# Causal attention scores at 64-key granularity: first half-blocks of two heads stacked in one score tile

## The chip, the cores and the metric

The kernel runs on one core of one Trainium2 chip. The metric is the device time of one execution in microseconds (us), the median over the runs of one kernel. The kernel before took 278.13 to 278.65 us in four runs. Every record calls its runs "fast", so all runs here are compared as they are; but runs of some changed kernels differ in their mean granted clock (split8: 0.987 to 1.0), and that is taken up below. Engines are called by their profile names: PE is TensorE, PEld its weight loads, ACT is ScalarE, DVE is VectorE, POOL is GpSimd, SP is SyncE, which only issues DMAs here.

## The reference, cut to what matters

A sequence of 2048 tokens of width 512 is cut into 4 segments of 512. Each of 32 heads (16 wide) does causal softmax attention inside a segment, plus a linear "memory" over the earlier segments; a gated MLP of width 1792 runs beside it, and a gate mixes the two.

```python
for s in range(4):
    logits = einsum('bhqd,bhkd->bhqk', qs, ks) * 0.25 + mask      # causal, inside the segment
    a_dot  = softmax(logits) @ vs
    a_mem  = (phi(qs) @ M) / (phi(qs) @ z + 1e-6)                 # phi(t) = t+1 if t>0 else exp(t)
    o = g * a_mem + (1 - g) * a_dot
    M, z = M + phi(ks).T @ vs, z + phi(ks).sum()
a = concat(o) @ wo
b = (gelu(x @ w_gate) * (x @ w_up)) @ w_down
out = gx * a + (1 - gx) * b                                       # gx = sigmoid(x . gate_w)
```

## The kernel before

The kernel is a list of tasks. A list scheduler inside the program orders them with estimated durations (`est`) and hand-tuned priorities (`BIAS`); each engine then runs its own part strictly in that order, and waits on semaphores where it needs another engine. So a change of a task's engine or of a buffer's name can move the whole order.

Scores for one group `t` of eight heads (four row groups `g` of 32 rows, two heads `j` in each) are written to one PSUM tile of 128 keys x 4 x 512 columns. `kpad[j]` is K with the rows of the other head set to zero. A "fill" is one set of tiled matmuls into that tile; one ACT instruction then takes exp of all 2048 columns, and POOL zeroes what lies above the diagonal.

```python
R_PT = 7                                   # buffers for exp(scores)
def fill(name, steps, diags):              # ... cut
    for (j, kb, ncol, c0) in steps:        # kb: block of 128 keys; queries from the block on
        for g in range(4):
            X[g][:, c0:c0+ncol] = kpad[j][32*g:32*g+32, t, kb*128:(kb+1)*128].T @ qT[32*g:..., t, kb*128:512]
    PT[slot] = exp(XALL * 0.25)            # ACT, 128 x 2048
    affine_select(PT[slot] ...)            # POOL, 512 or 1024 elements a partition

a0 = fill("A0", [(0, 0, 512, 0)], [0])
b0 = fill("B0", [(0, 1, 384, 0), (0, 3, 128, 384)], [0, 384])
cc = fill("C",  [(0, 2, 256, 0), (1, 2, 256, 256)], [(0, 256)])
a1 = fill("A1", [(1, 0, 512, 0)], [0])
b1 = fill("B1", [(1, 1, 384, 0), (1, 3, 128, 384)], [0, 384])
pv(0, a0, b0, cc, joint); pv(1, a1, b1, cc, joint)    # 16 tiled matmuls each: P times [V | 1]
norm()                                                # DVE: divide, transpose, add
```

That is 5 fills for each of 16 groups, 80 in all. Between them PE runs the projections and the MLP, whose 512-column matmuls fill four PSUM banks that ACT and DVE must empty. Other DVE work: `phi` of q and k (bf16 `tensor_scalar` from SBUF to SBUF: `phq`, `kT`, `pex`), the padded copies of K, and the eviction of every MLP tile.

The softmax here doesn't subtract the row's maximum and nothing guards it: scores larger than these inputs give would overflow.

## Time and profile before

| | before |
|---|---|
| time, median of 4 runs | 278.25 us (278.13 to 278.65) |
| profiled span | 276.7 us |
| PE / ACT / DVE / POOL busy | 265.9 / 213.1 / 196.7 / 101.5 us |
| matmuls of 512 columns start apart | 0.216 us |

The page's head and its rows of 40 slices: a digit is the busy share of a slice in tenths, and PEclk is the granted PE clock.

```profile
span 276.7 us, 5333 instructions
PE 265.9 (96%) x2147; PEld 114.8 (41%) x2186; DVE 196.7 (71%) x336; ACT 213.1 (77%) x166; POOL 101.5 (37%) x197
...
PE   8999999999999999999999999999899999999995
...
PEclk9999999999999999999999999999999999999999
```

PE never rests for long. What a fill costs PE is read from starts in the timeline of PE (start us, length us, what):

```profile
102.57 0.59 PE L430 MATMUL psW<-xT,wq 128*128 128x512 bf16 x2
103.09 0.40 PE L741 MATMUL psXALL<-qT,kpad_1 32*128 32x384 bf16 x8
103.42 0.61 PE L430 MATMUL psW<-xT,wq 128*128 128x512 bf16 x2
```

The second of the two full matmuls started at about 102.78, the next full one at 103.42: 0.64 us, of which a normal matmul would have taken 0.216. The fill costs PE 0.42 us, though its 512 columns stream in about 0.21.

Groups of POOL and DVE instructions (busy us, mean ns of one, idle time before them):

```profile
L761 POOL TENSOR_SCALAR_AFFINE_SELECT pt<-pt 128x512 bf16<-128x512 bf16 x96 | 63.7, 664 | 141.7 <-ACT pt L749 119.7 <-ACT exs L645 19.3
L761 POOL TENSOR_SCALAR_AFFINE_SELECT pt<-pt 128x1024 bf16<-128x1024 bf16 x16 | 17.6, 1101 | 14.3 <-ACT pt L749 14.3
...
L606 DVE TENSOR_SCALAR pex<-pex 128x1024 bf16<-128x1024 bf16 x12 | 5.9, 488 | 0.0
...
L604 DVE TENSOR_SCALAR phq<-qT 128x1024 bf16<-128x1024 bf16 x6 | 3.2, 529 | 0.0
```

### The profile page before, as it was taken

The page shows a single profiled execution, that of the slowest core. Times are in us where ns is not written, and L with a number is a line of the kernel's source. Part 1 is how long each engine was busy: PE and PEld are TensorE (multiplying, and loading weights), DVE is VectorE, ACT ScalarE, POOL GpSimd, SP SyncE. Part 2 cuts the span into 40 slices and gives each one's busy share as a digit, 9 for nine tenths or more (in the row PEclk, how much of TensorE's full clock was granted, in tenths as well). Part 3 has the DMA queues.
Part 4 walks back from the last instruction along what each step waited for, and adds up shares of the span by engine and source line. Part 5 has one row for each costly group of instructions (what it writes and reads, how often), then busy time and mean ns, then how long its engine had stood idle before and what let it go on. Part 6 is the DMA issues. An engine that isn't in the chain of part 4 may idle for free.

```text
span 276.7 us, 5333 instructions
## 1 busy us (share of the span) xinstructions
PE 265.9 (96%) x2147; PEld 114.8 (41%) x2186; DVE 196.7 (71%) x336; ACT 213.1 (77%) x166; POOL 101.5 (37%) x197
## 2 busy tenths in 40 slices
PE   8999999999999999999999999999899999999995
PEld 3444344334454434444454444433344334433342
DVE  1589879977889669989727999868553669273534
ACT  3698889899989779877778988767868668677701
POOL 8465633431013342464205543443300433342410
PEclk9999999999999999999999999999999999999999
DMA  6999940000022431000201210410000000001002
GB/s 177 217 376 361 201 79 2 0 4 0 0 59 57 95 40 59 1 2 10 50 0 21 57 40 0 97 38 1 4 0 0 4 0 2 19 21 39 0 2 76
DMA packets 29697, 15.30 MB, mean 55 GB/s; under 512 B 21224, under 2 KB 29672, under 8 KB 29672
## 3 DMA queue, kind: packets, MB, share of 16 engines
q1 hardware_dynamic: 29672, 14.96, 22.4%
q8 instruction: 17, 0.28, 0.4%
q14 instruction: 8, 0.07, 0.1%
HBM read 8.14 MB, written 2.10 MB: 37 GB/s over the span
## 4 chain that ended last, share of the span: by engine, by line
PE 81%; ACT 6%; DVE 4%; POOL 2%; issue 2%; DMA 2%; SPq 1%; DVEq 0%; ACTq 0%; POOLq 0%
PE psW L430 65%; PE psXALL L741 8%; PE psW L774 6%; ACT pt L749 5%; DMA wq<-in_A_wq_dram 2%; PE psXALL L430 1%; POOL exsT L656 1%; SPq L461 1%; POOL pt L761 1%; DVE hT L873 1%; ACT L852 1%; DVE ost L901 1%; DVE tb L782 0%; ACT hT L852 0%; DVE ndsc L678 0%
## 5 line engine op out<-in xcount | busy, mean ns | idle before, releaser
L749 ACT ACTIVATE pt<-psXALL 128x2048 bf16<-128x2048 f32 x80 | 150.1, 1877 | 39.0 <-PE psXALL L741 23.8
L761 POOL TENSOR_SCALAR_AFFINE_SELECT pt<-pt 128x512 bf16<-128x512 bf16 (+1 forms) x112 | 81.1, 727 | 156.0 <-ACT pt L749 134.0
L430 PE MATMUL psW<-xT,wu 128*128 128x512 bf16 x216 | 51.3, 380 | 1.4 <-DVE hT L873 0.6
L430 PE MATMUL psW<-wd,hT 128*128 128x512 bf16 x199 | 50.3, 380 | 1.2 <-issue 1.0
L430 PE MATMUL psW<-xT,wg 128*128 128x512 bf16 x216 | 50.3, 380 | 1.1 <-issue 0.8
L873 DVE TENSOR_TENSOR hT<-psW,hT 128x512 bf16<-128x512 f32 x56 | 37.3, 685 | 15.2 <-PE psW L430 13.6
L782 DVE STREAM_TRANSPOSE tb<-psW 128x512 f32<-128x512 f32 x32 | 21.1, 697 | 21.6 <-PE psW L774 21.4
L430 PEld LDWEIGHTS psW<-xT,wg 128*128 128x128 bf16 x224 | 20.5, 98 | 25.9 <-issue 2.6
L430 PEld LDWEIGHTS psW<-xT,wu 128*128 128x128 bf16 x224 | 20.2, 98 | 25.7 <-issue 2.6
L430 PEld LDWEIGHTS psW<-wd,hT 128*128 128x128 bf16 x210 | 18.7, 98 | 22.9 <-issue 4.0
L852 ACT ACTIVATE hT<-psW 128x512 bf16<-128x512 f32 x28 | 16.0, 600 | 6.8 <-PE psW L430 6.8
L774 PE MATMUL psW<-pt,vaug 128*17 128x256 bf16 (+3 forms) x512 | 20.4, 300 | 0.2 <-ACT hT L852 0.2
L430 PE MATMUL psW<-xT,wq 128*128 128x512 bf16 x59 | 15.7, 380 | 0.8 <-DMA wq<-in_A_wq_dram 0.3
L430 PE MATMUL psW<-xT,wk 128*128 128x512 bf16 x63 | 16.3, 380 | 0.2 <-issue 0.2
L741 PE MATMUL psXALL<-qT,kpad_1 32*128 32x512 bf16 (+3 forms) x256 | 15.8, 301 | 0.5 <-ACT pt L749 0.5
L741 PE MATMUL psXALL<-qT,kpad_0 32*128 32x512 bf16 (+3 forms) x256 | 15.8, 301 | 0.0
L430 PE MATMUL psW<-wv,xT 128*128 128x512 bf16 x61 | 15.4, 380 | 0.2
L447 DVE CAST hT<-psW 128x512 bf16<-128x512 f32 x20 | 13.1, 680 | 3.4 <-PE psW L430 3.4
L430 PE MATMUL psW<-wo,oT 128*128 128x512 bf16 x57 | 15.1, 380 | 0.2
L656 POOL COPY exsT<-exs 32x4 f32<-32x4 f32 x64 | 13.8, 216 | 3.7
L774 PEld LDWEIGHTS psW<-pt,vaug 128*17 128x17 bf16 x512 | 10.7, 90 | 10.5 <-issue 3.5
L901 DVE TENSOR_SCALAR ost<-psW,omgt 128x512 bf16<-128x512 f32 x10 | 7.3, 748 | 9.8 <-PE psW L430 9.8
(90 smaller groups left out, 252.1 us busy)
## 6 DMA issues: line engine op xcount, KB each, us to landing
out_dram<-ost SPq DMA_DIRECT2D x16, 128.0 KB, 1.7
wg<-in_B_w_gate_dram SPq DMA_DIRECT2D x2, 896.0 KB, 6.9
wu<-in_B_w_up_dram SPq DMA_DIRECT2D x2, 896.0 KB, 11.1
wd<-in_B_w_down_dram SPq DMA_DIRECT2D x1, 1792.0 KB, 15.9
hT<-in_A_x_dram SPq DMA_DIRECT2D x2, 256.0 KB, 3.0
wv<-in_A_wv_dram SPq DMA_DIRECT2D x1, 512.0 KB, 6.4
wo<-in_A_wo_dram SPq DMA_DIRECT2D x1, 512.0 KB, 12.7
wk<-in_A_wk_dram SPq DMA_DIRECT2D x1, 384.0 KB, 5.0
```

What stands on the lines that cost most here:

```text
L430: return Instr(lambda e: e.matmul(view(), lhsT, rhs, start=first, stop=last), reads=reads, writes=[fkey if fkey is not None else g.key], e ...
L447: alts[DVE] = [Instr(lambda e: e.tensor_copy(dst(), src()), reads=reads, writes=writes, est=dve_t(n))]
L461: return e.dma_start(out_ap(), in_ap())
L656: cross = task(f"exsT{s}", POOL, [Instr(lambda e, g=g, c=c: e.tensor_copy(exsT[sl][32 * g:32 * g + 32, c:16:4], exs[32 * c:32 * c + 32, s4 ...
L741: instrs.append(Instr(lambda e, t=t, g=g, j=j, kb=kb, ncol=ncol, c0=c0: e.matmul(X[g][:, c0:c0 + ncol], kpad[j][sl][32 * g:32 * g + 32, t, ...
L749: prev_exp[0] = exp_task(s, f"exp{s}_{t}{name}", [Instr(lambda e: e.activation(PT[slot][:], XALL[:, :].rearrange("p (g c) -> p g c", g=4), ...
L761: minstrs.append(Instr(lambda e, view=view, pat=pat: e.affine_select(out=view, in_=view, compare_op=ALU.is_ge, fill=0.0, base=0, pattern=p ...
L774: instrs.append(Instr(lambda e, q=q, kb=kb, slot=slot, c0=c0, h=h: e.matmul(gp.f32()[32 * q:32 * q + 17, 128 * kb:512], Vaug[sl][:, kb, h, :],
L782: task(f"pvt{s}_{t}_{j}", DVE, [Instr(lambda e: e.transpose(Tb[:, j, :], gp.f32()[:, :]), [gp.key], [("Tb", j)], dve_t(512))], grp=gp)
L852: lambda e, g=g, ft=ft, s=s: e.activation(hT[s % 2][:, ft, :], g.f32()[:, :], ACTF.Gelu_apprx_tanh),
L873: task(f"Um{s}_{ft}", DVE, [Instr(lambda e, g=g, ft=ft: e.tensor_tensor(hT[sl][:, ft, :], g.f32()[:, :], hT[sl][:, ft, :], ALU.mult), [g.k ...
L901: DVE: [Instr(lambda e, view=view, gt=gt, tile=tile: e.tensor_scalar(ostage[tile][:], view(), omgt[:, gt:gt + 1], None, ALU.mult), rd, [(" ...
```

## The change

The intent is to waste fewer score columns. In the old fills, the first 64 queries of a 128-key block are computed against all 128 keys, though causality allows only the first 64. The change lets the row fills start at query 64 of each block, and gathers the left-out corners (64 keys x 64 queries) of two heads, stacked on 128 partitions, of all four blocks and of two groups `t` in one extra "low" fill. 4 x 16 + 8 = 72 fills instead of 80, so 72 exps of 2048 columns. For the low part, a second V operand `Vlow[j]` holds V of the first 64 keys on one half of the partitions and zeros on the other; a DMA brings it across partitions. Room for the new tiles comes from other buffers, and all priorities (`BIAS`) were tuned anew.

```diff
-R_PT = 7
+R_PT = 6
+N_OST = 3                                   # output stages, were 4
+    klow = sb("klow", [P, 4, 4, 2, 64])      # first 64 keys of each block, both heads, padded
-    pex = [sb(f"pex{i}", ...) for i in range(2)]
+    pex = sb("pex", [P, 2, 512])
+    Vlow = [sb(f"vlow{j}", [P, 4, 16, 17]) for j in range(2)]
-    otok = sb("otok", [P, 4, 512])           # obf and ott: also 2 -> 1
+    otok = sb("otok", [P, 2, 512])
+    PTl = sb("ptl", [P, 4, 512])             # exp of the low fill, one buffer
+        for j in range(2):
+            dma(f"Vlo{s}_{j}", SP, lambda j=j: Vlow[j][64*j:64*j+64], lambda j=j: Vaug[sl][0:64, :, j], ...)
+            def rows(j, kbs, name):          # key blocks (0,3) and (1,2): 448+64 and 320+192 columns
+                ... kpad[j] block kb x queries kb*128+64 .. 512; masks of 256 elements
+            def lows():                      # 2 groups x 4 blocks x 64 columns
+                masks = [(PTl[64 * h:64 * h + 64].rearrange("p g (b c) -> p (g b) c", c=64),
+                          [[0, 32], [1, 64]], 0, 2048) for h in range(2)]
+                fill("L", steps, PTl, ("PTl",), masks)
             def pv(...):                     # 16 matmuls of 448,320,192,64 columns
+                for kb in range(4):          # and 16 of 64 columns
+                    for q in range(4):
+                        ... Vlow[j][:, kb, 4*t+q, :] x PTl[:, q, 256*(t%2)+64*kb : +64]
-            a0, b0, cc, a1, b1 = five fills
+            for j in range(2):
+                at[j] = {**rows(j, (0, 3), f"A{j}"), **rows(j, (1, 2), f"B{j}")}
+                if j == 0 and t % 2 == 0:
+                    lows()
```

The mask of the low fill is two POOL selects, one for each half of the partitions, of 2048 elements each.

## The prediction

> **What bounds the kernel now.** TensorE. The page gives PE busy 265.9 of 276.7 us (96%), ACT 213.1, DVE 196.7, POOL 101.5. In the windows view only about 6 us of idle PE lie between 10 and 263 us. The chain of waits is 81% PE; where it passes through exp and masking (114 to 129, 246 to 253 us) PE is full of other matmuls. So the time is the sum of PE's start-to-start intervals plus a few us of stalls. ACT is the second limit: in the timeline the score tile cycles every 2.59 us (fill, exp of 1.877, fill), 80 x 2.59 = 207 us.
>
> **What changes, from start-to-start intervals in the trace.**
> - Fills. A fill among full matmuls takes 0.311 us from the last full start to its own and 0.329 to the next full one; less the 0.216 of a normal matmul it costs 0.424, with 4 matmuls or with 8. Half is a fixed price of switching. Eight fewer: -3.4 us. The 64 row fills keep 512 columns and 8 matmuls: unchanged.
> - The 8 low fills have 32 matmuls of 64 columns. Four tiled matmuls start 3 to 4 ns apart, which agrees with the Trainium skill, "TensorE: Matmul & The Clock Gate", Part 3 (about 4 ns), so four fit into the 27 ns that 64 columns stream. Part 1 puts a floor of about 25 ns under start-to-start; the trace agrees (one-column gate matmuls start 25 ns apart). 64 columns are just above it. Estimate: 3 to 10 ns extra per step, +0.2 to +0.6 us in all.
> - PV. 1280 columns per accumulation before and after; matmuls double, 512 to 1024. Steps of 512, 384, 256, 128 columns now take 222, 163, 109, 56 ns: streaming plus about 4. Four more steps: +15 to +50 ns for each of 32, +0.5 to +1.5 us.
> - PV runs that start after full matmuls, not behind a fill, fall from 4 to 2 in the instruction order: -0.6 us.
> - ACT: 8 exps fewer, -15 us; off the critical path, except that some of 2 to 3 us of mid-kernel PE stalls may go.
> - POOL: 112 masks (0.664 us for 512 elements, 1.10 for 1024) become 128 of 256 (estimate 0.44) and 16 of 2048 (estimate 2.0): 81 to 88 us. The low mask is two in a row, 4 us of latency before a pair's first PV.
> - DVE: klow copies, +5 us. DMA: 8 small copies of V. Six P tiles for seven, single low P and V buffers, three output stages: more possible waits. All off the critical path if the order has room.
>
> **Predicted time.** PE: -3.4 + 0.4 + 1.0 - 0.6 = -2.6 us. Stalls: even, give or take 2. About **275.6 us**, 8 in 10 between 272.8 and 279.2. Faster by over 2%: 0.09; within 2%: 0.85; slower: 0.06. The 15 us taken from ACT almost all become ACT idle.
>
> **What the profile should show.** PE 95 to 97% busy; ACT busy 198 to 200 us; 72 exps of 1.88; a fill still 0.42 us of PE, a low fill 0.42 to 0.51; a PV accumulation 0.56 to 0.60 us instead of 0.55, its short steps 29 to 37 ns; POOL 100 to 115 us; fill cycle still 2.6 us.
>
> **What would make it wrong.** Slower: short steps of 50 ns or more because weight loads can't keep up (+2.5 us or more for PV, +1.5 for low fills); PV waiting for the low mask or for the single low buffers, with PE standing; a copy of V blocking transposes behind it in the queue. Faster: stalls that vanish with ACT's new slack, up to 3 us more.

## The result, and the profile after

The changed kernel took 285.9 us (285.69 to 287.6, 4 runs) beside 278.25 us. Ratios in this document are the mean time of one kernel's runs over that of the other's of the same rounds, so not quite the ratio of the medians. Here it is 1.0286, with a 95% interval of 1.0245 to 1.0327: slower by 2.9%, and outside the predicted range. The output is correct.

The same lines of the page:

```profile
span 284.3 us, 6936 instructions
PE 264.7 (93%) x2913; PEld 120.8 (42%) x2954; DVE 196.8 (69%) x338; ACT 206.1 (72%) x170; POOL 115.1 (40%) x231
...
PE   8999859989999989999999969997999999999995
...
PEclk9999999999999999999999989997999999999999
```

PE has less busy time and a longer span: holes appear, and the clock row has two dips. From the matmul records, the gaps of PE above 0.5 us are one of 0.6 us before, and six after: 0.93 (at 28.9 us), 2.73 (36.9), 0.99 (60.1), 1.14 (104.4), 2.55 (164.4) and 1.78 (193.3), together 10.1 us.

The PE costs themselves were as predicted. A PV pair of the changed kernel:

```profile
72.35 0.61 PE L810 MATMUL psW<-pt,vaug 128*17 128x448 bf16 x16
72.79 0.29 PE L818 MATMUL psW<-ptl,vlow 128*17 128x64 bf16 x16
72.91 0.61 PE L810 MATMUL psW<-pt,vaug 128*17 128x448 bf16 x16
```

From start to start one accumulation takes 0.56 us; before it took 0.55. The steps of 64 columns run 29 ns apart (median), and a low fill costs 0.45 us of PE against 0.43 for a row fill (medians).

What changed is elsewhere. Groups of POOL and DVE (smaller and other groups between them are left out, here and below):

```profile
L768 POOL TENSOR_SCALAR_AFFINE_SELECT pt<-pt 128x256 bf16<-128x256 bf16 x128 | 57.4, 451 | 139.8 <-ACT pt L764 115.8 <-ACT exs L665 18.3
L768 POOL TENSOR_SCALAR_AFFINE_SELECT ptl<-ptl 64x2048 bf16<-64x2048 bf16 x16 | 34.5, 2157 | 9.7 <-ACT ptl L764 9.1
...
L612 DVE TENSOR_SCALAR pex<-pex 128x1024 bf16<-128x1024 bf16 x12 | 11.1, 924 | 4.5 <-ACT pex L607 4.5
L644 DVE TENSOR_SCALAR klow<-kT,maskc 128x1024 bf16<-128x1024 bf16 x6 | 6.5, 1131 | 0.0
L610 DVE TENSOR_SCALAR phq<-qT 128x1024 bf16<-128x1024 bf16 x6 | 5.8, 963 | 0.0
```

The very same `pex` and `phq` instructions take almost twice as long on average. The timelines of POOL and of DVE around the first gap show why:

```profile
23.58 4.42 POOL L768 TENSOR_SCALAR_AFFINE_SELECT ptl<-ptl 64x2048 bf16<-64x2048 bf16 x2 [0.69 <-ACT ptl L764]
```

```profile
24.36 1.68 DVE L610 TENSOR_SCALAR phq<-qT 128x1024 bf16<-128x1024 bf16 x1
25.96 2.33 DVE L612 TENSOR_SCALAR pex<-pex 128x1024 bf16<-128x1024 bf16 x1
28.33 0.77 DVE L614 TENSOR_TENSOR phq<-phq,pex 128x1024 bf16<-128x1024 bf16 x1
29.02 1.27 DVE L452 CAST hT<-psW 128x512 bf16<-128x512 f32 x2
```

The two selects ran from 23.584 to 25.755 and from 25.823 to 28.009 us. `phq` ended at 26.041 and `pex` at 28.292: each 0.28 to 0.29 us after the end of the select that was running when it started. Two such instructions at 161 to 165 us give the same 0.28 us. It is not `tensor_scalar` alone: a `tensor_tensor` between SBUF tiles (L845), 0.42 to 0.43 us elsewhere, took 1.47 us under a select at 190.1 us. The nine evictions from PSUM that ran wholly under a low select were not held: 677 to 692 ns, 690 elsewhere (median). But DVE runs in the order of its list, so the PSUM eviction behind the two came about 3 us late (1.27 and 1.92 us over the 0.41 of a free one), and PE stood for a bank (timeline of PE):

```profile
27.00 1.90 PE L435 MATMUL psW<-xT,wg 128*128 128x512 bf16 x8
29.84 0.59 PE L435 MATMUL psW<-xT,wg 128*128 128x512 bf16 x2 [0.93 <-DVE hT L452]
```

At 36.9 us PE waits for something else, the first copy of V:

```profile
36.31 0.61 PE L810 MATMUL psW<-pt,vaug 128*17 128x448 bf16 x16
39.66 0.29 PE L818 MATMUL psW<-ptl,vlow 128*17 128x64 bf16 x16 [2.73 <-DMA vlow<-vaug]
```

And after the gap at 164.4 us five full matmuls take 2.34 us, so 0.43 us apart, twice the normal 0.216. The windows view of that stretch, and of the one with the gap at 193.3 us (length in us; busy us and count of PE, PEld, DVE, ACT, POOL; mean clock; DMA share, GB/s) gives the clock as 0.90 and 0.89:

```profile
168.00 2.34 PE L435 MATMUL psW<-wo,oT 128*128 128x512 bf16 x5
```

```profile
155.00:172.00 17.00, 14.24 (x118) 5.84 (x114) 14.79 (x25) 11.47 (x10) 11.21 (x25) 0.90 0.16 32
185.00:200.00 15.00, 13.00 (x172) 5.70 (x163) 11.42 (x17) 8.71 (x6) 6.82 (x8) 0.89 0.15 38
```

The trace's clock record has two stretches of 3.413 us at half clock, which by our estimate cost about 1.7 us of PE work each (half of 3.413).

The longest gap, 2.73 us, brought no such stretch, so length alone does not decide. The clock record changes only on a grid of 3.413 us. On this grid, in all 14 profiles, each of the eleven full-clock windows in which PE stood for 1.78 us or more was followed by half clock, and no window with 1.68 us or less was. The 2.73 us fell across two windows, 1.36 and 1.38 us.

### The profile page after: what moved, and what is told of

The parts are those of the page before. It is cut to its first block, busy times and chain, and to the rows that moved or that the text cites. A ratio compares the mean times of both kernels' runs of the same rounds, so it can differ in the third digit from the quotient of the medians.

```text
span 284.3 us, 6936 instructions
## 1 busy us (share of the span) xinstructions
PE 264.7 (93%) x2913; PEld 120.8 (42%) x2954; DVE 196.8 (69%) x338; ACT 206.1 (72%) x170; POOL 115.1 (40%) x231
## 4 chain that ended last, share of the span: by engine, by line
PE 75%; DVE 15%; issue 3%; ACT 3%; POOL 2%; DMA 1%; SPq 0%; ACTq 0%; POOLq 0%
PE psW L435 60%; PE psXALL L757 7%; PE psW L810 5%; DVE hT L452 3%; DVE pex L612 3%; POOL exsT L676 2%; DVE phq L610 1%; PE psXALL L435 1%; ACT pt L764 1%; DVE klow L644 1%; PE psW L818 1%; PE psW L518 1%; DMA vlow<-vaug 1%; DVE phq L614 1%; DVE tb L825 1%
## 5 line engine op out<-in xcount | busy, mean ns | idle before, releaser
L764 ACT ACTIVATE pt<-psXALL 128x2048 bf16<-128x2048 f32 x64 | 120.1, 1876 | 44.3 <-PE psXALL L757 39.7
L768 POOL TENSOR_SCALAR_AFFINE_SELECT pt<-pt 128x256 bf16<-128x256 bf16 x128 | 57.4, 451 | 139.8 <-ACT pt L764 115.8
L435 PE MATMUL psW<-xT,wu 128*128 128x512 bf16 x216 | 53.1, 388 | 2.7 <-DVE otok L708 1.8
L435 PE MATMUL psW<-wd,hT 128*128 128x512 bf16 x201 | 49.1, 380 | 1.2 <-issue 1.1
L768 POOL TENSOR_SCALAR_AFFINE_SELECT ptl<-ptl 64x2048 bf16<-64x2048 bf16 x16 | 34.5, 2157 | 9.7 <-ACT ptl L764 9.1
L810 PE MATMUL psW<-pt,vaug 128*17 128x192 bf16 (+3 forms) x512 | 18.8, 273 | 0.0
L764 ACT ACTIVATE ptl<-psXALL 128x2048 bf16<-128x2048 f32 x8 | 15.0, 1876 | 3.1 <-PE psXALL L757 3.1
L435 PE MATMUL psW<-wo,oT 128*128 128x512 bf16 x54 | 16.2, 410 | 0.6 <-issue 0.5
L452 DVE CAST hT<-psW 128x512 bf16<-128x512 f32 x21 | 14.0, 681 | 1.9 <-PE psW L435 1.7
L612 DVE TENSOR_SCALAR pex<-pex 128x1024 bf16<-128x1024 bf16 x12 | 11.1, 924 | 4.5 <-ACT pex L607 4.5
```

The lines of the kernel that those rows point to most:

```text
L435: return Instr(lambda e: e.matmul(view(), lhsT, rhs, start=first, stop=last), reads=reads, writes=[fkey if fkey is not None else g.key], e ...
L452: alts[DVE] = [Instr(lambda e: e.tensor_copy(dst(), src()), reads=reads, writes=writes, est=dve_t(n))]
L612: Instr(lambda e: e.tensor_scalar(ex[:], ex[:], 1.0, None, ALU.min), [("pex",)], [("pex",)], dve_t(1024, 4)),
L764: prev_exp[0] = exp_task(s, f"exp{s}_{t}{name}", [Instr(lambda e: e.activation(dst[:], XALL[:, :].rearrange("p (g c) -> p g c", g=4), ACTF ...
L768: m = task(f"msk{s}_{t}{name}", POOL, [Instr(lambda e, view=view, pat=pat, base=base: e.affine_select(out=view, in_=view, compare_op=ALU.i ...
L810: instrs.append(Instr(lambda e, t=t, q=q, kb=kb, slot=slot, c0=c0: e.matmul(gp.f32()[32 * q:32 * q + 17, 128 * kb + 64:512], Vaug[sl][:, k ...
```

## The experiments

Theory A: a POOL select of 2.16 us holds off DVE's fast SBUF-to-SBUF instructions until it ends; DVE evicts late, PE stands, and the clock drops after some of the longer gaps. The Trainium skill, "SBUF — State Buffer", section "Who interferes with whom", says that VectorE and GpSimd share a pair of SBUF ports, that a VectorE instruction in a two-port mode contends for it, and that whoever comes first has it for the whole instruction. The trace agrees (1.68 and 2.33 us for instructions of 0.41). Rival B: the smaller number of buffers, and the V copy in the DMA queue.

Twelve kernels ran. All gave correct results. "Order unchanged" was checked by comparing the instruction lists of each engine. The diffs below are cut to what matters, and some are shortened in words.

| kernel | median us | range | ratio to before (95%) |
|---|---|---|---|
| changed kernel | 285.90 | 285.69 to 287.60 | 1.0286 (1.0245 to 1.0327) |
| split16 | 278.80 | 278.24 to 279.21 | 1.0010 (0.9992 to 1.0028) |
| split8 | 277.82 | 276.20 to 279.22 | 0.9974 (0.9922 to 1.0026) |
| before_lock | 285.64 | 284.12 to 285.74 | 1.0244 (1.0215 to 1.0273) |
| before_bufs | 324.24 | 323.45 to 324.80 | 1.1650 (1.1625 to 1.1674) |
| before_fixbufs | 283.73 | 283.52 to 283.83 | 1.0187 (1.0169 to 1.0204) |
| before_split | 277.66 | 277.29 to 277.79 | 0.9975 (0.9962 to 0.9988) |
| dvemask | 296.89 | 294.61 to 298.24 | 1.0647 (1.0611 to 1.0683) |
| dvemask_fix | 277.20 | 276.02 to 279.07 | 0.9968 (0.9936 to 0.9999) |
| split8_vlo | 277.64 | 275.29 to 279.39 | 0.9972 (0.9931 to 1.0013) |
| dvemask_vlo | 276.34 | 275.39 to 278.43 | 0.9941 (0.9908 to 0.9975) |
| after_q | 281.92 | 280.04 to 283.31 | 1.0128 (1.0088 to 1.0168) |
| dvemask_q | 273.91 | 272.82 to 274.01 | 0.9828 (0.9809 to 0.9847) |

### split8 and split16: the same masks in shorter pieces

```diff
-                masks = [(PTl[64*h:64*h+64].rearrange("p g (b c) -> p (g b) c", c=64),
-                          [[0, 32], [1, 64]], 0, 2048) for h in range(2)]
+                masks = [(PTl[64*h:64*h+64].rearrange("p g (b c) -> p (g b) c", c=64)[:, 8*i:8*i+8],
+                          [[0, 8], [1, 64]], 0, 0) for h in range(2) for i in range(4)]   # split16: 16 blocks, 2 pieces
```

The estimates keep their sum, so PE, DVE, ACT and SP run in the same order.

> The changed kernel with each of the 16 low masks (2048 elements, 2.16 us) cut into four of 512 elements; the order of instructions on every other engine is the same, and the POOL work is not less (about 0.66 us x 64 = 42 us for 34.5). Theory A (a long POOL instruction holds off the vector engine's fast SBUF-to-SBUF instructions for up to 2.3 us, evictions come late, TensorE stands): no such vector instruction over 1.3 us, TensorE's long gaps mostly go, 279 to 282 us. Rival B (fewer and single buffers, and the V copy in the queue): no gain, 285.5 to 288 us, since the low mask takes longer, not shorter.

> The same, each low mask cut into two of 1024 elements (1.1 us). Theory A: a dose between, 281 to 284 us, vector instructions held up to about 1.5 us. Rival B: 285.5 to 287 us.

POOL of split8, then its DVE `tensor_scalar` groups:

```profile
L768 POOL TENSOR_SCALAR_AFFINE_SELECT ptl<-ptl 64x512 bf16<-64x512 bf16 x64 | 45.5, 711 | 13.0 <-ACT ptl L764 9.0
```

```profile
L612 DVE TENSOR_SCALAR pex<-pex 128x1024 bf16<-128x1024 bf16 x12 | 7.5, 621 | 1.9 <-ACT pex L607 1.9
L610 DVE TENSOR_SCALAR phq<-qT 128x1024 bf16<-128x1024 bf16 x6 | 3.4, 568 | 0.0
```

POOL works 11 us longer on the low masks (45.5 for 34.5 us), and the kernel is 8.1 us faster. So it is the length of one POOL instruction that costs, not POOL's total and not the time until the low mask is done, which got longer (from the end of the exp mostly 4.4 to 5.0 us in the changed kernel, 5.8 to 7.0 here). Rival B alone cannot explain that. Both ranges were missed on the good side: even pieces of 1.22 us (split16) win back 7.1 us. In split8's profile PE's gaps above 0.5 us shrink to two, 2.01 us at 36.7 us and 0.68. Split8's four runs lie apart, 276.2 and 276.7 at a clock of 1.0, and 278.9 and 279.2 at 0.994 and 0.987: in half of the runs the clock still drops. The 2.01 us gap is the likely cause, though only one run has a trace: there it fell across two windows of the grid (0.33 and 1.68 us) and the clock stayed full.

### before_lock: the kernel before, with long POOL instructions added

```diff
+    scr = sb("scr", [P, 1536], mybir.dt.uint8)          # nothing else reads it; its memset is cut here
+                if name == "C" and t % 2 == 0:
+                    for _ in range(2):
+                        v = scr[0:64, :]
+                        minstrs.append(Instr(lambda e, v=v: e.affine_select(out=v, in_=v, compare_op=ALU.is_ge,
+                            fill=0.0, base=4096, pattern=[[1, 1536]], channel_multiplier=-1), [("scr",)], [("scr",)], 0.0))
```

> The kernel before with 16 extra POOL selects of 64 x 1536 bytes on a scratch tile that nothing reads, two after the C mask of every even head group, where the changed kernel has its low masks; nothing else moves in any engine's order. Theory A: fast vector instructions held for up to about 1.7 us, 280.5 to 285 us. Rival B: 278 to 279 us.

The 16 useless selects take 1.55 us each, and the kernel loses 7 us, a little over the 6.7 us that the expectation allowed. The same DVE group as above went from 488 to 735 ns:

```profile
L769 POOL TENSOR_SCALAR_AFFINE_SELECT scr<-scr 64x1536 uint8<-64x1536 uint8 x16 | 24.8, 1553 | 0.5
```

```profile
L608 DVE TENSOR_SCALAR pex<-pex 128x1024 bf16<-128x1024 bf16 x12 | 8.8, 735 | 0.0
```

Long POOL selects in those places are thus enough to cost 7 us, with no low fill, no V copy and all buffers in place. The half clock is not needed for it: the run at a clock of 1.0 took 285.58 us. The selects also hold up the real masks behind them in POOL's order, but the trace shows no stop of PE's matmuls over 0.1 us that ended with POOL, and PE's weight loads waited for POOL as long as before (1.2 us). The stops that ended with DVE went from 2.4 us in the kernel before to 7.1 us. The longest (timelines of POOL, DVE and PE):

```profile
89.36 3.25 POOL L769 TENSOR_SCALAR_AFFINE_SELECT scr<-scr 64x1536 uint8<-64x1536 uint8 x2
```

```profile
89.61 1.68 DVE L608 TENSOR_SCALAR pex<-pex 128x1024 bf16<-128x1024 bf16 x1
91.32 1.83 DVE L610 TENSOR_TENSOR kT<-kT,pex 128x1024 bf16<-128x1024 bf16 x1
```

```profile
93.81 0.41 PE L431 MATMUL psW<-mzbd,phq 128*128 128x128 bf16 x4 [1.98 <-DVE otok L690]
```

### before_bufs and before_fixbufs: the buffers alone

```diff
-R_PT = 7
+R_PT = 6
+N_OST = 3
-    pex = [sb(f"pex{i}", [P, 2, 512]) for i in range(2)]
+    pex = sb("pex", [P, 2, 512])                        # and otok 4 -> 2, obf and ott 2 -> 1
```

> The kernel before with the changed kernel's buffer counts only: 6 P tiles, 3 output stages, one exp buffer for q and k, two token tiles, single normalisation tiles. Theory A: 278 to 280.5 us. Rival B (buffers cost it): 283 us or more.

It took 324 us, which answers nothing: with other buffers the scheduler made another order. In its chain of waits PE runs 154 plain matmuls without a break from 25.97 us, and then stands between exps:

```profile
25.97 30.85 PE psW L431 x154
...
62.02 1.89 ACT pt L750
63.95 0.50 PE psXALL L742 x4
64.53 1.89 ACT pt L750
```

The repair keeps the old order and renames the buffers only after scheduling, when the waits are made. The old order has two `pex` tiles in flight at once, so that one stays double.

```diff
+    def phys(k):                                        # after scheduling, before the waits are planned
+        if k[0] in ("obf", "ott"): return (k[0],)
+        if k[0] == "PT":   return ("PT", k[1].n % 6 ...)
+        if k[0] == "otok": return ("otok", k[1] % 2)
+        if k[0] == "ost":  return ("ost", k[1] % 3)
```

> The kernel before in its own order of instructions on every engine, with 6 P tiles instead of 7, 3 output stages, two token tiles and single normalisation tiles; only the exp buffer for q and k stays double, since the old order does not allow one. This repairs before_bufs, in which the order moved too. Theory A (long POOL instructions are the cost): 278 to 279.5 us. Rival B (buffer counts cost it): 281 us or more.

283.7 us, so fewer buffers do cost the old kernel 5.2 us (1.9%) in an order that was made for more of them, and theory A's number was wrong here. But the changed kernel, whose order was tuned for its own buffers, wins back its whole loss with these buffers in place once the masks and the queue are mended: it reaches 273.9 us at the end of this section. Whether more buffers would win it still more, and which of the four kinds costs the old kernel those 5 us, was not tried.

### dvemask and dvemask_fix: no long POOL instruction at all

```diff
+    m01 = sb("m01", [P, 64])                            # 1 where query >= key, for both halves
-   two POOL affine_selects of 64 x 2048
+   e.tensor_tensor(v, v, m01 broadcast over 32 blocks, ALU.mult)     # DVE, v = the whole low tile
```

> The changed kernel with the low mask as one vector multiply by a 0/1 tile (8 of them, about 1.2 us each) instead of two POOL selects of 2.16 us. POOL falls to about 80 us busy, DVE gains 10 us, no POOL instruction over 0.5 us is left in the attention part; orders move, as the scheduler knows the task's new engine. Theory A: 275 to 278 us, no fast vector instruction held for more than about 0.6 us. Rival B: 281 us or more, as the buffers and the V copy are still there.

296.9 us, far outside what was expected. The mask is not to blame: the multiply took 1.22 us, as estimated. But the task now belonged to DVE, the scheduler placed everything anew, and from 200 to 217 us the chain of waits consists almost only of exps and the fills between them, with little other PE work. From 195 to 220 us the mean PE clock was 0.72:

```profile
195.00:220.00 25.00, 14.45 (x177) 5.98 (x176) 11.60 (x20) 14.16 (x9) 4.52 (x11) 0.72 0.05 12
```

The lesson is about method: in this kernel an experiment has to hold the order. dvemask_fix lets the scheduler see the POOL task as before, and puts the multiply into DVE's stream afterwards.

```diff
     for t in S.schedule():
+        if t in low_on_dve:
+            em.plan(DVE, low_on_dve[t])
+            continue
```

> The changed kernel in its own order on TensorE, ScalarE and the queue; each low mask is one vector multiply (1.22 us in the last run) put into the vector engine's order where the POOL selects stood. This repairs dvemask, in which the whole order moved. Theory A: no long POOL instruction is left, 275.5 to 278.5 us, though 10 us more of vector work. Rival B (buffers and the V copy, in the order that was tuned for them): 283 us or more.

277.2 us, 8.7 less than the changed kernel, in its own PE and ACT order and with its own buffers. It agrees with theory A and is out of rival B's range. DVE's busy time fell from 196.8 to 188.8 us although it took over 9.8 us of multiplies. In its profile one PE gap above 0.5 us is left: 1.98 us at 37.0 us, the wait for the V copy.

### before_split: a control

```diff
-  one select of 4 x 128 (or 8 x 128) elements
+  selects of 256 elements, same order, same sum of estimates
```

> Control: the kernel before with all its masks in pieces of 256 elements (0.45 us instead of 0.66 and 1.10), order unchanged. Theory A says that its own masks hold the vector engine a little too, but that no chain hangs on it: 277.5 to 279.5 us (shorter holds against about 20 us more POOL work).

277.66 us: a gain of 0.25% with an interval that excludes zero, so the old masks of 0.66 and 1.10 us hold DVE too (its busy time fell from 196.7 to 188.9 us), but nothing much hangs on it. The gain of the splits above is therefore not a gift that any mask splitting would bring.

### split8_vlo and dvemask_vlo: the V copy, first try

The last gap is a wait for the first segment's copy of V. V was evicted at about 22 us; the copy was issued at 36.3 us, since SP issues in order (the queue's timeline, dvemask_fix):

```profile
18.22 8.58 SPq L463 DMA_TRANSPOSE xT<-in_A_x_dram  x1
26.85 3.29 SPq L463 DMA_TRANSPOSE phkt<-kT  x2
30.18 4.68 SPq L463 DMA_TRANSPOSE xT<-in_A_x_dram  x3
34.90 1.26 SPq L463 DMA_TRANSPOSE phkt<-kT  x1
36.28 1.36 SPq L467 DMA_DIRECT2D vlow<-vaug  x2
```

```diff
-    for t in S.schedule():
+    order = S.schedule()
+    for t in [t for t in order if t.name.startswith("Vlo0_")]:
+        order.remove(t)
+        order.insert(1 + max(order.index(p) for p in t.preds), t)
+    for t in order:
```

> split8 with the two V copies of the first segment issued as soon as V is there, ahead of the transposes that they stood behind. If the copy is what is left of the loss, the 2 us wait of the first PV for it goes: 274.5 to 276.5 us, and the runs at a clock below 1.0 become rare. If not: as split8, 276 to 279.

> Both: low masks on the vector engine in the fixed order, and the first V copies early. 274 to 276.5 us if both waits were real and independent; this should be the best version of the changed kernel.

The move was too short. In the profiles it took the copies past one of the seven transposes shown above (the expectation for dvemask_q below says two of eight); six stayed in front, the copies still went out at 35.8 and 36.0 us, and the gap stayed (2.84 us in the profile of dvemask_vlo, 3.93 in that of split8_vlo). split8_vlo is as split8; dvemask_vlo's 276.3 us cannot be told from dvemask_fix. These two runs also show what spreads the times. By run, dvemask_vlo took 275.4 to 275.6 us at a clock of 0.998 to 1.0, and 277.1 to 278.4 us at 0.992 to 0.994.

### dvemask_q and after_q: the V copy, second try

```diff
+    order = S.schedule()                     # as above, and then:
+    late = [t for t in order[:at] if re.match(r"(x2|pkT0)_", t.name)]     # the transposes in front
+    ... removed, and put back behind the two copies
```

> dvemask_fix with the two V copies of the first segment issued before the eight transposes that they stood behind (the last run moved them past two only, and they still went out at 35.8 us, though V was there at 22 us). If the copy's place in the queue is what is left: the 2.0 to 2.8 us gap of TensorE near 37 us goes, the clock stays at 1.0 in nearly all runs, 273.5 to 275.5 us. If the gap only moves to another wait: 275.5 to 278 us.

> The changed kernel with the queue repair alone, long POOL masks as they were. Splits the loss between the two: theory A says the masks are the larger part, 282 to 284.5 us (2 to 3 us less); if the copy were the main part, under 280 us.

dvemask_q took 273.9 us, 1.7% under the kernel before (0.9809 to 0.9847); all five runs had a clock of 0.999 or 1.0, and no PE gap above 0.5 us is left. The queue, the place of the old gap, and the page:

```profile
22.57 3.50 SPq L467 DMA_DIRECT2D vlow<-vaug  x2
```

```profile
36.36 0.62 PE L821 MATMUL psW<-pt,vaug 128*17 128x448 bf16 x16
36.80 0.29 PE L829 MATMUL psW<-ptl,vlow 128*17 128x64 bf16 x16
```

```profile
PE 262.1 (96%) x2913; PEld 121.2 (45%) x2954; DVE 189.0 (69%) x346; ACT 205.9 (76%) x170; POOL 82.5 (30%) x218
```

after_q, the queue repair without the mask repair, took 281.9 us, just under the 282 to 284.5 expected. So the two causes can be set out as a square of ratios to the kernel before:

| | V copy as it was | V copy early |
|---|---|---|
| POOL masks of 2.16 us | 1.0286 | 1.0128 |
| mask on DVE | 0.9968 | 0.9828 |

The masks cost 3.0 to 3.2% of 278 us (8.3 to 8.8 us), the queue 1.4 to 1.6% (about 4 us), and the two add up. Both figures contain clock. after_q's runs fall in two groups, 280.0 to 280.9 us at a clock of 1.0 and 283.0 to 283.3 at 0.987 to 0.988, while no run of the changed kernel was above 0.988. Between runs of like clock the queue repair is worth 2.6 to 2.7 us (285.8 against 283.2 us at 0.987 to 0.988, 276.3 against 273.7 at 0.999 to 1.0), and the mask repair 6.9 us (280.5 against 273.7 at full clock); the rest goes with half clock.

## Why the prediction was wrong

- **The PE sum was right in its parts.** A low fill 0.45 us (predicted 0.42 to 0.51), a PV accumulation 0.56 us (0.56 to 0.60), short steps 29 ns (29 to 37). The feared failure, weight loads that cannot keep up with 64 columns, did not happen.
- **The step that failed** is "All off the critical path if the order has room", and with it the term "Stalls: even, give or take 2". PE's gaps above 0.5 us went from 0.6 to 10.1 us, and half clock took another 3.4 us. In the page's figures the span grew by 7.6 us: idle PE by 8.8 (10.8 to 19.6 us), less 1.2 us of PE busy time (265.9 to 264.7). This busy time contains the 3.4 us of half clock, so without it PE worked about 4.6 us less. The saving came, but idle time and half clock (12.2 us) were far larger.
- **What was missed in it.** The prediction costed the low mask as POOL time and as latency for PV. It did not ask what a POOL instruction of 2 us does to DVE. It even had the sizes, "16 of 2048 (estimate 2.0)"; measured 2.16. The before_lock run shows that long selects alone take 7 us, and the split runs that the same masks in pieces win back 7 to 8 us.
- **The V copy was named, but the wrong way round**: "a copy of V blocking transposes behind it in the queue". The copy was the one that stood behind transposes. Putting it in front was worth about 4 us (2.6 to 2.7 between runs of like clock).
- **PV waiting for the low mask** was named as a risk and was not the main thing: in the changed kernel no stop of PE's matmuls over 0.1 us ended with POOL, and split8 made the mask later and the kernel faster.
- **ACT** fell to 206.1 us, not 198 to 200. The eight exps did go (120.1 + 15.0 us for 150.1); the new order gave ACT more evictions instead. PE at 93% contradicted "95 to 97%", as it should have where stalls were mis-sized.
- With both waits repaired, the same idea gives 273.9 us, 4.5 us under the kernel before, where the prediction's PE sum said 2.6. By the pages, PE's busy time fell by 3.8 us (265.9 to 262.1) and its idle time by 0.7 (10.8 to 10.1). So PE saved 1.2 us more than the sum said; from which of its terms, or from what in the new order, is not shown. (The two traces lack nearly the same number of matmul records, 39 and 41.)

## What to carry to other kernels

Before giving POOL a long instruction, look at which DVE instructions of the fast SBUF-to-SBUF kind will run meanwhile, and what waits behind them: the length of one POOL instruction counts, not POOL's total, and cutting it in pieces, or doing it on DVE, can be worth more than the work it adds. For each new DMA look up what stands in front of it in its queue, and not only whether its data are ready. And where a scheduler decides the order, hold the order fixed in an experiment, or the answer is about the order.

## What the Trainium skill lacked or had wrong

- "SBUF — State Buffer", "Who interferes with whom", is right about the lock, but gives no number for a GpSimd select against VectorE. Here eight bf16 `tensor_scalar` instructions of 128x1024, 0.41 us when free, took 1.68 to 2.34 us under selects of 2.1 to 2.2 us, and each ended 0.28 to 0.29 us after a select did.
- "TensorE: Matmul & The Clock Gate", "Why this matters for your kernels", asks for no PE gap over about 3 us to keep the clock. Here gaps of 2.55 and 1.78 us (changed kernel) were each followed by one stretch of half clock, while gaps of 2.58 and 1.78 us at the same places of after_q were not. What told them apart in all 14 profiles was the idle time within one window of the clock's grid: 1.78 us or more brought half clock, 1.68 us or less did not. The length of the stretch, 3.413 us, agrees with the window that Part 1 states.
- The same page, Part 1, says that starts never come closer than about 25 ns. That holds for untiled matmuls (25 ns at one column). Tiled ones start 2 to 5 ns apart (Part 3 says about 4), and a step of four with their weight loads took 29 ns at 64 columns.
- No page gives the price of a switch between full and tiled matmuls (it would belong to "TensorEngine Tiling (Array Packing)"): a tiled fill of 512 columns cost 0.42 us of PE, about twice its streaming time of 0.21.
